# Linear attention feeding a gated feed-forward block: the first pairs reordered across queues and PSUM banks

## The chip, the cores and the metric

The kernel runs on one core of one Trainium2 chip. Five engines with queues of their own work on it: TensorE (PE: matrix products; PEld is its weight load), VectorE (DVE), ScalarE (ACT), GpSimd (POOL, used here for set-up only) and SyncE (SP), which issues every DMA. The metric is device time in microseconds. Three runs of the kernel before took 1288.86, 1289.1 and 1289.23 us, a median of 1289.1 us.

## The reference

Q, K and V have 8 batches of 8 heads, 576 positions and 64 features, in float32; `w_phi` is 64 by 128. Positive random features are made of Q and K, attention is linear, and its output, 4608 tokens of 512 features, passes a feed-forward block of width 1536.

```python
def phi(x):
    proj = einsum('bhsd,df->bhsf', x, w_phi)
    proj = proj - max(abs(proj), axis=-1)
    return concatenate([exp(proj), exp(-proj)], axis=-1)
q_p, k_p = phi(q), phi(k)
kv  = einsum('bhsf,bhsd->bhfd', k_p, v)
z   = sum(k_p, axis=2)
num = einsum('bhsf,bhfd->bhsd', q_p, kv)
den = einsum('bhsf,bhf->bhs', q_p, z)[..., None] + 1e-06
x   = (num / den), heads side by side: 4608 x 512
out = (sigmoid(x @ w_gate) * (x @ w_val)) @ w_out
```

## The kernel before

**Stages.** A pair is two heads of one batch; there are 32 pairs in `steps`, four to a batch. Stage 1 does the attention of all pairs, and between their steps the feed-forward block for the first 4 of 12 slices of its width (`JA`), in 18 chunks of 256 tokens. Its sums go to DRAM (`yscr`). Stage 2 (`rest_chunks`) does the other 8 slices in nine chunks of 512 tokens and adds the stored part. In the feed-forward block each operand is split into a high and a low part (`xh`, `xl`, `wh`, `wl`, `hh`, `hl`), and each product is three matmuls.

**Who sets the order.** In stage 1 everything runs in the order in which the Python code emits it, on each engine by itself (`manual_schedule`). Work that needs several engines in turn is written as generators: `start(g)` runs one to its first `yield`, `tick()` moves every running generator on by one step. What a generator emits in a later tick stands further back in its engine's queue.

**One pair.** `keys` (L477) projects K for two heads into two PSUM banks (L423) and starts `k_exp` (L429): the largest absolute value (`mx`, L434), the subtraction (`dk`, L447) and two exponentials per head on ScalarE (`ek`, L456), one step each. `q_half` (L404), called twice, projects half of Q (L413), and `copies` has ScalarE bring it to `d` (L475). `rest` (L481) does the 64 last positions of both heads (L484) and, from pair `EARLY` = 4 on, lets VectorE add the exponentials of K over three of the position tiles first (`k_sum`, L461: `s` at L469 and `su` at L470, twice a pair). `q_max` (L494) takes the largest absolute value of Q's features on VectorE: a transposing reduction (`pm`, L502), small copies across partitions (`pn`, L507 to L513), a transpose back (`mb`, L515) and the subtraction in `d` (L520). `q_exp` (L560) makes both exponentials (L566). `kv` (L522) accumulates K's features with V (40 matmuls, L530) and the sum z (L544: 40 matmuls from the exponentials, or 16 from `su`) in one bank, which ScalarE copies out (`kvt`, L549). `turn` (L552) transposes it (L556) and copies it out (`kv`, L558). `num` (L571) multiplies with Q's features (`nm`, L582), and for the denominators (`dp`, L593); ScalarE copies the results (`ex`, L599, and `dr`, L609).

**Normalising.** `norm` (L612) sends the denominators through a DMA to a narrow tile, adds 1e-6 and takes reciprocals there, stores them to DRAM (`dens`) and loads them back spread over the partitions (`rb`), each step some ticks after the one before. `num(i, True)` ("soon") instead makes them from `dp` at once, in a tile of full width (L604, L605); before, only pair 3 does. `scale` (L633) multiplies, and stores the result (`xscr`). For batch 0 it also writes the split of x straight into the first chunks' tiles (`split`, L61), and no load follows.

**Banks.** PSUM has eight banks here: two in `ps_gv` for gate and value products, one in `ps_acc` for the output sums, five in `ps_a`. Before, every attention product takes one of the five from `ps_a` (`bank`, L364), and a bank comes free when its last reader has passed.

**The loops.** The first loop (L731) runs pairs 0 to 3 with no feed-forward work. The main loop (L759) starts with the projections of pair 4 and calls `fill` four times a step. `fill` counts spots, adds to `due` what a spot should carry (what is `ready`, spread over the spots left, at most `RATE`), and emits units as `due` allows, with three ticks each time. A unit is half a gate product (`half`, L239) or an output sum (`half_out`, L254); `gate` (L219) is its part on ScalarE and VectorE (L226 to L236). `queue(b)` (L708) makes batch b's chunks due `LAG` spots later. `half` waits, by ticking, until its chunk's x and its weights have been emitted. `weigh` (L669) turns the weights of 12 tiles from 64-bit numbers to high and low parts by `weight_tile` (L121), as far as `grant` allows. After the last pair the remaining units follow without attention between them (L789).

Of the kernel before, what the change touches and what calls it, by code (L numbers as in the profile page):

```python
# [36 lines left out]
EARLY = NP  # L37
RATE = 2.8
LAG = (2, 8)
# [5 lines left out]
def attention_moe(  # L45
# [75 lines left out]
    def weight_tile(w, raw, mid, wp, sp):  # L121
        j, m = divmod(w, 3)
        n = f"{j}_{m}"
        if m == 0:
            weights[j] = tuple(
                wp.tile([P, 3 * DM], F32R, tag=f"w{x}{j}", name=f"w{x}{j}") for x in "hl"
            )
        h, l = (x[:, m * DM : m * DM + DM] for x in weights[j])
        hi = raw.rearrange("p (n two) -> p n two", two=2)[:, :, 1]
        words = mid.rearrange("p (n two) -> p n two", two=2)  # L130
        rest, unit = words[:, :, 0], words[:, :, 1]
        top = sp.tile([P, DM], U32, tag="wtop", name="wtop" + n)
        vec.tensor_scalar(top, hi, 0x7FFFFE00, None, op0=ALU.bitwise_and)
        act.activation(top, top, AF.Relu, bias=ebias, scale=8.0)
        vec.tensor_scalar(rest, rest, 0x01FFFFFF, None, op0=ALU.bitwise_and)
        yield
        vec.scalar_tensor_tensor(
            top, hi, 0x80000000, top, op0=ALU.bitwise_and, op1=ALU.bitwise_or
        )
        nc.sync.dma_start(h.bitcast(U32), top)  # L140
        yield
        vec.tensor_scalar(unit, top, 0xFF800000, None, op0=ALU.bitwise_and)
        vec.scalar_tensor_tensor(
            l, rest, 2.0**-36, unit.bitcast(F32), op0=ALU.mult, op1=ALU.mult
        )
# [208 lines left out]
    with ExitStack() as actx:  # L354
# [9 lines left out]
        def bank(shape, name):  # L364
            return ps_a.tile(shape, F32, tag="a", name=name)
# [14 lines left out]
        steps = [(b, p) for b in range(B) for p in range(NP)]  # L380
# [23 lines left out]
        def q_half(i, hf):  # L404

            n = f"{i}_{hf}"
            if hf == 0:
                ds[i] = at.tile([P, 2, S], F32, tag="d", name=f"d{i}")
# [9 lines left out]
        def k_heads(i):  # L418
            kx = loaded["k", i]
            pps = [bank([P, 4, F], f"pk{i}_{hd}") for hd in range(2)]  # L420
# [60 lines left out]
        def rest(i):  # L481
# [4 lines left out]
            def go():  # L486
                yield from k_exp(i, (2,), [pp], 1)
                if i >= EARLY:
                    yield
                    yield from k_sum(i)  # L490
# [3 lines left out]
        def q_max(i):  # L494
# [6 lines left out]
            mb = at.tile([P, 2, S], F32, tag="mb", name=f"mb{i}", bufs=1)  # L501
# [12 lines left out]
            yield  # L514
            vec.transpose(  # L515
# [6 lines left out]
        def kv(i):  # L522
# [3 lines left out]
            kvz = bank([P, 3 * F], f"kvz{i}")  # L526
# [25 lines left out]
        def turn(i):  # L552
            kvt = kvs[i]
            tp = bank([P, 3, P], f"tp{i}")
# [5 lines left out]
        def q_exp(i):  # L560
            yield
            d = ds.pop(i)
            es = []
            for sg in range(2):
                e = at.tile([P, 2, S], F32, tag=f"eq{sg}", name=f"eq{i}_{sg}", bufs=1)
                act.activation(e, d, AF.Exp, scale=1.0 - 2.0 * sg)  # L566
                es.append(e)
                yield
            exps[i] = es

        def num(i, soon=False):  # L571
# [5 lines left out]
            dps = [bank([P, HS], f"dp{i}_{hf}") for hf in range(1 + soon)]  # L577
            for hf in range(2):
                cs = slice(hf * HS, hf * HS + HS)
                for sg in range(2):  # L580
                    for o in range(0, P, Q):
# [4 lines left out]
                        )  # L586
            for n, dp in enumerate(dps):
# [10 lines left out]
            for hf in range(2):  # L598
                act.copy(ex[:, hf * HS : hf * HS + HS], nms[hf])  # L599
            if soon:  # L600
                rb = at.tile([P, S], F32, tag="mb", name=f"rb{i}", bufs=1)
                for hf, dp in enumerate(dps):
                    cs = slice(hf * HS, hf * HS + HS)
                    vec.tensor_scalar(rb[:, cs], dp, 1e-6, None, op0=ALU.add)  # L604
                    vec.reciprocal(rb[:, cs], rb[:, cs])  # L605
                start(scale(i, ex, rb))
# [5 lines left out]
        def norm(i, ex, dr):  # L612
# [16 lines left out]
            for _ in range(4):  # L629
                yield  # L630
            yield from scale(i, ex, rb)

        def scale(i, ex, rb):  # L633
            b, p = steps[i]
            xp = at.tile([P, S], F32, tag="xp", name=f"xp{i}")
            vec.tensor_tensor(xp, ex, rb, op=ALU.mult)
            for c in range(S // CH if b == 0 else 0):
# [3 lines left out]
                ps = slice(p * CH, p * CH + CH)  # L641
                split(xs[c][0][:, ps], xs[c][1][:, ps], xp[:, c * CH : c * CH + CH])
                parts[c] += 1
            yield
# [80 lines left out]
        N = len(steps)  # L725
# [5 lines left out]
        for i in range(-1, EARLY):  # L731
            load(i + 2 if i >= 0 else N)
            if i + 1 < EARLY:
                keys(i + 1)
                copies(q_half(i + 1, 0))
                tick()
                tick()
                copies(q_half(i + 1, 1))
                rest(i + 1)
                start(q_max(i + 1))  # L740
                tick()
                tick()
            if i >= 0:
                kv(i)
                start(q_exp(i))
            if i >= 1:
                num(i - 1)
            tick()
            tick()
# [121 lines left out]
```

## Time and profile before

| | us |
|---|---|
| median of three runs | 1289.1 |
| the profiled execution's own time | 1289.85 |
| its span, first to last instruction | 1288.1 |
| TensorE busy in the span | 1221.7 |
| VectorE busy | 798.1 |
| ScalarE busy | 525.4 |
| mean granted TensorE clock, share of full | 0.973 |

The profile is one execution. Its first part gives each engine's busy time; its second cuts the span into 40 slices of 32.2 us, where a digit is a busy share in tenths. Groups of instructions stand by line, engine and tile, with their shapes, count, busy time, mean duration in ns, and the engine's idle time just before them with the instruction that ended it. A tile name on the left of an arrow is written, those on the right are read. One matmul call of float32 operands can show as several instructions, so the counts of L413 and L423 are twice those of the calls. Matmuls overlap, so one matmul's duration is longer than its share of the time; in the chain of waits the pieces do not overlap.

### The profile page before, as it was taken

The numbers are of one execution on the slowest core, as the hardware profiler recorded it, in microseconds if no ns is written. First come the engines' busy times: TensorE is split into PE (matmuls) and PEld (weight loads), VectorE is DVE, ScalarE is ACT, GpSimd is POOL, SyncE is SP. The second block draws the span as 40 slices with busy tenths as digits, with TensorE's granted clock in tenths as the row PEclk, the third lists the DMA queues.
The fourth block names the chain that finished last, engine by engine and source line by source line (L and its number), as shares of the span: only waits on it lengthen the run. The fifth ranks groups of instructions, "written<-read, shape, count | busy, mean of one in ns | idle before, by whom it ended". The sixth has DMA issues, their size and how long they took to land.

```text
span 1288.1 us, 22464 instructions
## 1 busy us (share of the span) xinstructions
PE 1221.7 (95%) x9120; PEld 964.7 (75%) x9120; DVE 798.1 (62%) x1608; ACT 525.4 (41%) x1081; POOL 0.7 (0%) x6
## 2 busy tenths in 40 slices
PE   6847799999999999999899999999999999999998
PEld 4435566777787777776798888888888888888886
DVE  7699887888878778884796943434342434333333
ACT  5535556565655656664444322222122222222221
POOL 0000000000000000000000000000000000000000
PEclk8968899999999999999899999999999999999999
DMA  4556334333442433431674530302020201111010
GB/s 176 181 185 236 104 108 138 114 118 105 137 129 84 129 108 110 119 116 58 240 236 169 192 98 1 99 1 92 8 84 15 67 31 57 42 44 56 9 58 33
DMA packets 80869, 131.55 MB, mean 102 GB/s; under 512 B 18301, under 2 KB 37885, under 8 KB 80765
## 3 DMA queue, kind: packets, MB, share of 16 engines
q1 hardware_dynamic: 80764, 130.11, 31.3%
q8 instruction: 72, 1.18, 0.4%
q14 instruction: 33, 0.26, 0.1%
HBM read 92.04 MB, written 28.45 MB: 94 GB/s over the span
## 4 chain that ended last, share of the span: by engine, by line
PE 81%; DVE 10%; ACT 3%; DMA 3%; issue 2%; SPq 0%; DVEq 0%; ACTq 0%
PE acc L171 21%; PE g L164 15%; PE v L164 15%; PE gv L164 11%; PE kvz L530 5%; PE nm L582 4%; PE pq L413 2%; PE dp L593 2%; PE pk L423 2%; ACT eq L566 1%; PE kvz L544 1%; DMA wraw<-w_moe 1%; PE pk L484 1%; DMA rb<-den 1%; DVE t L231 1%
## 5 line engine op out<-in xcount | busy, mean ns | idle before, releaser
L164 PE MATMUL gv<-xh,wh 128*128 128x256 f32 x576 | 173.1, 301 | 14.7 <-ACT xh L62 11.9
L171 PE MATMUL acc<-wh,hh 128*128 128x512 f32 x432 | 172.0, 398 | 0.7 <-ACT hh L234 0.7
L171 PE MATMUL acc<-wl,hh 128*128 128x512 f32 x432 | 169.1, 391 | 0.0
L164 PE MATMUL gv<-xl,wh 128*128 128x256 f32 x576 | 166.2, 289 | 2.8 <-DVE xl L211 2.8
L171 PE MATMUL acc<-wh,hl 128*128 128x512 f32 x432 | 168.7, 390 | 0.0
L164 PE MATMUL gv<-xh,wl 128*128 128x256 f32 x576 | 165.6, 287 | 0.0
L183 DVE TENSOR_SCALAR t<-t 128x512 uint32<-128x512 uint32 x72 | 30.7, 426 | 171.8 <-ACT t L180 171.7
L164 PEld LDWEIGHTS gv<-xh,wh 128*128 128x128 f32 x576 | 112.8, 196 | 32.0 <-issue 14.9
L62 ACT CAST hh<-u 128x512 fp32r<-128x512 f32 x72 | 44.6, 619 | 219.2 <-DVE u L185 219.2
L180 ACT ACTIVATE t<-g 128x512 f32<-128x512 f32 x72 | 43.0, 597 | 183.9 <-PE g L164 183.8
L164 PEld LDWEIGHTS gv<-xl,wh 128*128 128x128 f32 x576 | 113.0, 196 | 3.8 <-DVE xl L211 3.0
L164 PE MATMUL g<-xh,wh 128*128 128x512 f32 x288 | 113.0, 392 | 0.0
L164 PEld LDWEIGHTS gv<-xh,wl 128*128 128x128 f32 x576 | 113.0, 196 | 0.0
L164 PE MATMUL v<-xh,wh 128*128 128x512 f32 x288 | 112.6, 391 | 0.0
L164 PE MATMUL g<-xh,wl 128*128 128x512 f32 x288 | 112.5, 391 | 0.0
L164 PE MATMUL g<-xl,wh 128*128 128x512 f32 x288 | 112.5, 391 | 0.0
L164 PE MATMUL v<-xl,wh 128*128 128x512 f32 x288 | 112.3, 390 | 0.0
L164 PE MATMUL v<-xh,wl 128*128 128x512 f32 x288 | 112.1, 389 | 0.0
L184 DVE SCALAR_TENSOR_TENSOR t<-t,v 128x512 f32<-128x512 f32 x72 | 49.4, 686 | 97.9 <-PE v L164 97.9
L171 PEld LDWEIGHTS acc<-wh,hh 128*128 128x128 f32 x432 | 81.1, 188 | 22.4 <-issue 4.8
L171 PEld LDWEIGHTS acc<-wh,hl 128*128 128x128 f32 x432 | 81.1, 188 | 18.7 <-DVE hl L236 0.2
L171 PEld LDWEIGHTS acc<-wl,hh 128*128 128x128 f32 x432 | 81.3, 188 | 16.0
(92 smaller groups left out, 2114.1 us busy)
## 6 DMA issues: line engine op xcount, KB each, us to landing
wraw<-w_moe SPq DMA_DIRECT2D x36, 512.0 KB, 5.7
xl<-xs SPq DMA_DIRECT2D x34, 512.0 KB, 4.1
k<-k SPq DMA_DIRECT2D x32, 320.0 KB, 3.7
v<-v SPq DMA_DIRECT2D x32, 320.0 KB, 3.0
q<-q SPq DMA_DIRECT2D x32, 288.0 KB, 4.3
wh<-wtop SPq DMA_DIRECT2D x36, 256.0 KB, 2.3
ys<-y SPq DMA_DIRECT2D x36, 256.0 KB, 2.0
yp<-ys SPq DMA_DIRECT2D x36, 256.0 KB
```

What stands on the lines that cost most here:

```text
L62: a = act.copy(h, x)
L164: nc.tensor.matmul(o, a[:, ws], x[:, cs], start=i == 0, stop=i == 11)
L171: nc.tensor.matmul(acc, a[:, ts], w[:, ws], start=first and i == 0, stop=last and i == 2)
L180: act.activation(t, g, AF.Tanh, scale=0.5)
L183: vec.tensor_scalar(tu, tu, 0x7FFFFFFF, None, op0=ALU.bitwise_and)
L184: vec.scalar_tensor_tensor(t, t, 1.0, vl, op0=ALU.add, op1=ALU.mult)
L231: vec.scalar_tensor_tensor(t, t, 1.0, gv[:, 1, :], op0=ALU.add, op1=ALU.mult)
L413: nc.tensor.matmul(pps[hd], wk[head(hd), :], x[head(hd), cs], start=True, stop=True)
L423: nc.tensor.matmul(pps[hd][:, t, :], kx[head(hd), t * P : t * P + P], wk[head(hd), :], start=True, stop=True,)
L530: nc.tensor.matmul(kvz[o : o + Q, : 2 * F], vx[:, 2 * t + hd, o % D : o % D + Q], (e0, e1)[hd][:, t, :] if t < 4 else e2[:, 0, :], start=t ...
L582: nc.tensor.matmul(nms[hf][o : o + Q, :], w[:, sg, o : o + Q], es[sg][:, o // D, cs], start=sg == 0, stop=sg == 1, tile_position=(0, o),)
L593: nc.tensor.matmul(dp[o : o + Q, :], w[:, 2, z : z + Q], es[sg][:, hd, hf * HS : hf * HS + HS], start=sg == 0, stop=sg == 1, tile_position ...
```

## The change

- `ONPE` = 10: `k_sum` is used from pair 10 on instead of pair 4, so pairs 4 to 9 sum K's features with 40 matmuls.
- `LAG` goes from (2, 8) to (4, 8).
- `weight_tile` gains a step: the mask of `rest` is emitted ahead of the Relu, and the Relu one tick later.
- For the first pairs `bank` takes other pools: K's projections of pairs 0 to 4 the two gate banks, `kvz` and its transpose of pairs 0 to 3 the one output bank.
- `d` has three buffers. Q's second exponential is written over `d`, the first has two buffers. For pairs 0 to 3 `q_exp` emits both at once, right after the copies of the next pair, ahead of `kv`.
- `num` copies each half of `nm` as soon as its matmuls are emitted, and takes the banks of `dp` after that. With `soon`, the addition and the reciprocal are made in the bank, and `scale` multiplies from it.
- `norm` waits two ticks instead of four after loading `rb`, for pairs 0 to 3.
- `scale` casts x one tick after the product, and subtracts one tick after that.
- The first loop takes in the projections of pair 4 and pair 3's `num`; the main loop starts at pair 4. In its last two steps `fill` is called where the projections would stand. The last pair (31) is done with `soon`.

```diff
+ONPE = 10
-LAG = (2, 8)
+LAG = (4, 8)
...
         vec.tensor_scalar(top, hi, 0x7FFFFE00, None, op0=ALU.bitwise_and)
+        vec.tensor_scalar(rest, rest, 0x01FFFFFF, None, op0=ALU.bitwise_and)
+        yield
         act.activation(top, top, AF.Relu, bias=ebias, scale=8.0)
-        vec.tensor_scalar(rest, rest, 0x01FFFFFF, None, op0=ALU.bitwise_and)
         yield
...
-        def bank(shape, name):
+        def bank(shape, name, i=N, ps=None, tag=None):
+            if i < EARLY:
+                return ps.tile(shape, F32, tag=tag, name=name)
             return ps_a.tile(shape, F32, tag="a", name=name)
...
-                ds[i] = at.tile([P, 2, S], F32, tag="d", name=f"d{i}")
+                ds[i] = at.tile([P, 2, S], F32, tag="d", name=f"d{i}", bufs=3)
...
-            pps = [bank([P, 4, F], f"pk{i}_{hd}") for hd in range(2)]
+            pps = [bank([P, 4, F], f"pk{i}_{hd}", i - 1, ps_gv, "gv") for hd in range(2)]
...
-                if i >= EARLY:
+                if i >= ONPE:
                     yield
                     yield from k_sum(i)
...
-            kvz = bank([P, 3 * F], f"kvz{i}")
+            kvz = bank([P, 3 * F], f"kvz{i}", i, ps_acc, "acc")
...
-            tp = bank([P, 3, P], f"tp{i}")
+            tp = bank([P, 3, P], f"tp{i}", i, ps_acc, "acc")
...
         def q_exp(i):
-            yield
+            if i >= EARLY:
+                yield
             d = ds.pop(i)
-            es = []
-            for sg in range(2):
-                e = at.tile([P, 2, S], F32, tag=f"eq{sg}", name=f"eq{i}_{sg}", bufs=1)
-                act.activation(e, d, AF.Exp, scale=1.0 - 2.0 * sg)
-                es.append(e)
-                yield
-            exps[i] = es
+            e = at.tile([P, 2, S], F32, tag="eq", name=f"eq{i}")
+            act.activation(e, d, AF.Exp)
+            if i >= EARLY:
+                yield
+            act.activation(d, d, AF.Exp, scale=-1.0)
+            exps[i] = e, d
+            yield
...
+                act.copy(ex[:, cs], nms[hf])
+            dps = [bank([P, HS], f"dp{i}_{hf}") for hf in range(1 + soon)]
...
-            for hf in range(2):
-                act.copy(ex[:, hf * HS : hf * HS + HS], nms[hf])
             if soon:
-                rb = at.tile([P, S], F32, tag="mb", name=f"rb{i}", bufs=1)
-                for hf, dp in enumerate(dps):
-                    cs = slice(hf * HS, hf * HS + HS)
-                    vec.tensor_scalar(rb[:, cs], dp, 1e-6, None, op0=ALU.add)
-                    vec.reciprocal(rb[:, cs], rb[:, cs])
-                start(scale(i, ex, rb))
+                for dp in dps:
+                    vec.tensor_scalar(dp, dp, 1e-6, None, op0=ALU.add)
+                    vec.reciprocal(dp, dp)
+                start(scale(i, ex, dps))
                 return
...
-            for _ in range(4):
+            for _ in range(4 if i >= EARLY else 2):
                 yield
...
-            vec.tensor_tensor(xp, ex, rb, op=ALU.mult)
+            for n, rb in enumerate(rbs):
+                cs = slice(n * w, n * w + w)
+                vec.tensor_tensor(xp[:, cs], ex[:, cs], rb, op=ALU.mult)
+            if b == 0:
+                yield
...
-                split(xs[c][0][:, ps], xs[c][1][:, ps], xp[:, c * CH : c * CH + CH])
+                act.copy(
+                    xs[c][0][:, p * CH : p * CH + CH], xp[:, c * CH : c * CH + CH]
+                )
+            yield
+            for c in range(S // CH if b == 0 else 0):
+                xh, xl = (x[:, p * CH : p * CH + CH] for x in xs[c])
+                vec.tensor_tensor(
+                    xl, xp[:, c * CH : c * CH + CH], xh.bitcast(F32), op=ALU.subtract
+                )
                 parts[c] += 1
...
         for i in range(-1, EARLY):
             load(i + 2 if i >= 0 else N)
-            if i + 1 < EARLY:
-                keys(i + 1)
-                copies(q_half(i + 1, 0))
-                tick()
-                tick()
-                copies(q_half(i + 1, 1))
-                rest(i + 1)
-                start(q_max(i + 1))
-                tick()
-                tick()
+            keys(i + 1)
+            copies(q_half(i + 1, 0))
+            copies(q_half(i + 1, 1))
+            rest(i + 1)
+            start(q_max(i + 1))
+            tick()
             if i >= 0:
+                start(q_exp(i))
                 kv(i)
-                start(q_exp(i))
+            tick()
+            tick()
             if i >= 1:
                 num(i - 1)
-            tick()
-            tick()
             if i >= 0:
                 turn(i)
                 load_v(i + 2)
-            tick()
-            tick()
+            if i == EARLY - 1:
+                num(i, True)
+            for _ in range(3):
+                tick()
             grant(i)
-        num(EARLY - 1, True)
-        grant(6)
         queue(0)
-        for i in range(EARLY - 1, N + 1):
-            if EARLY <= i:
-                load(i + 2)
-                grant(3 * (i - 1))
+        for i in range(EARLY, N + 1):
+            load(i + 2)
+            grant(3 * (i - 1))
...
+            else:
                 fill()
-            if i < EARLY:
-                fill()
-                fill()
-                continue
+            fill()
             if i < N:
                 kv(i)
             if i > EARLY:
-                num(i - 1)
+                num(i - 1, i == N)
```

More of the change, by code (lines that the diff above doesn't have):

```diff
@@ L362, in attention_moe @@
         ps_acc = actx.enter_context(tc.tile_pool(name="ps_o", bufs=1, space=PSUM))
-        def bank(shape, name):
+        steps = [(b, p) for b in range(B) for p in range(NP)]
+        N = len(steps)
+        def bank(shape, name, i=N, ps=None, tag=None):
+            if i < EARLY:
+                return ps.tile(shape, F32, tag=tag, name=name)
             return ps_a.tile(shape, F32, tag="a", name=name)
@@ L379, in attention_moe @@
         ]
-        steps = [(b, p) for b in range(B) for p in range(NP)]
         loaded, ks, ds, exps, kvs, rbs = {}, {}, {}, {}, {}, {}
@@ L500, in q_max @@
             pn = at.tile([P, nj], F32, tag="pn", name=f"pn{i}")
-            mb = at.tile([P, 2, S], F32, tag="mb", name=f"mb{i}", bufs=1)
             vec.tensor_reduce(
@@ L514, in q_max @@
             yield
+            mb = at.tile([P, 2, S], F32, tag="mb", name=f"mb{i}", bufs=1)
             vec.transpose(
@@ L560, in q_exp @@
         def q_exp(i):
-            yield
-            d = ds.pop(i)
-            es = []
-            for sg in range(2):
-                e = at.tile([P, 2, S], F32, tag=f"eq{sg}", name=f"eq{i}_{sg}", bufs=1)
-                act.activation(e, d, AF.Exp, scale=1.0 - 2.0 * sg)
-                es.append(e)
-                yield
-            exps[i] = es
+            if i >= EARLY:
+                yield
+            d = ds.pop(i)
+            e = at.tile([P, 2, S], F32, tag="eq", name=f"eq{i}")
[4 more added lines that the diff above has]
+            exps[i] = e, d
+            yield
         def num(i, soon=False):
@@ L576, in num @@
             nms = [bank([P, HS], f"nm{i}_{hf}") for hf in range(2)]
-            dps = [bank([P, HS], f"dp{i}_{hf}") for hf in range(1 + soon)]
             for hf in range(2):
@@ L628, in norm, with scale @@
                 )
-            for _ in range(4):
+            for _ in range(4 if i >= EARLY else 2):
                 yield
-            yield from scale(i, ex, rb)
-        def scale(i, ex, rb):
+            yield from scale(i, ex, [rb])
+        def scale(i, ex, rbs):
             b, p = steps[i]
             xp = at.tile([P, S], F32, tag="xp", name=f"xp{i}")
-            vec.tensor_tensor(xp, ex, rb, op=ALU.mult)
+            w = S // len(rbs)
+            for n, rb in enumerate(rbs):
[3 more added lines that the diff above has]
+                yield
             for c in range(S // CH if b == 0 else 0):
@@ L640, in scale @@
                     xs[c] = x_tiles(moe, CH, f"1_{c}")[:2]
-                ps = slice(p * CH, p * CH + CH)
-                split(xs[c][0][:, ps], xs[c][1][:, ps], xp[:, c * CH : c * CH + CH])
+                act.copy(
[7 more added lines that the diff above has]
+                )
                 parts[c] += 1
-            yield
             t = 0
@@ L723, in grant @@
                 wdone += 1
-        N = len(steps)
         for i in range(2):
```

## The prediction, made before the change was run

> **What bounds the kernel now.** First the page: its span, and busy tenths and granted TensorE clock in 40 slices.
>
> ```profile
> span 1288.1 us, 22464 instructions
> PE   6847799999999999999899999999999999999998
> DVE  7699887888878778884796943434342434333333
> PEclk8968899999999999999899999999999999999999
> ```
>
> TensorE (PE) is busy nearly everywhere from the sixth slice (160 us) on; only the first five slices show holes, a lower clock, and VectorE (DVE) at 6 to 9 tenths. The windows view puts numbers on it (columns: length, busy us of PE, weight loads, VectorE, ScalarE, GpSimd; granted clock, DMA share, GB/s).
>
> ```profile
> 17.80:66.92 49.12, 40.12 (x614) 24.40 (x614) 36.32 (x73) 29.53 (x61) 0.00 (x0) 0.92 0.42 139
> 66.92:164.50 97.58, 68.75 (x665) 49.02 (x666) 87.66 (x192) 47.90 (x108) 0.00 (x0) 0.80 0.55 177
> 0.00:164.50 164.50, 116.81 (x1331) 79.22 (x1332) 134.88 (x289) 83.25 (x181) 0.70 (x6) 0.84 0.53 175
> 164.50:240.00 75.50, 70.37 (x732) 49.76 (x731) 60.46 (x130) 44.95 (x98) 0.00 (x0) 0.95 0.42 124
> 240.00:280.00 40.00, 40.00 (x471) 30.25 (x474) 33.44 (x77) 24.32 (x57) 0.00 (x0) 1.00 0.38 119
> ```
>
> From 240 us TensorE is the bound without a hole, so what happens there costs or saves exactly its TensorE work. Before 164.5 us TensorE idles 164.5 - 116.81 = 47.7 us. In 66.92 to 164.5 VectorE is busy 87.66 of 97.58 us, 90%: **it is the bound there**. In 17.8 to 66.92 it idles 12.8 us. The waits view of TensorE, 60 to 160 us, names who comes last.
>
> ```profile
> PE pq L413 <- ACT d L475: 14.6, 5, 5.3
> PE gv L164 <- ACT xh L62: 11.9, 2, 8.4
> PE kvz L530 <- issue: 3.1, 1, 3.1
> ```
>
> The 11.9 us are the first MoE halves (a half: the 12 matmuls of one gate or value product), placed in the code ahead of pair 4's attention, waiting for pairs 3 and 2 to be normalised and cast. The 14.6 us are Q's projections waiting for a PSUM bank that ScalarE (ACT) has not copied out, ScalarE itself standing behind something VectorE makes.
>
> **A checkpoint.** I take the end of `d -= max` (L520) of pair 8. The windows view of L520, then that of L164, to 164.5 us:
>
> ```profile
> 0.00:164.50 164.50, 12.19 (x9) 0.84 0.53 175
> 0.00:164.50 164.50, 27.34 (x157) 24.07 (x158) 0.84 0.53 175
> ```
>
> The ninth L520 is pair 8's and ends at 164.5 us; by then 157/12 = 13.1 MoE halves have started. All 12 weight tiles are cast by it in both kernels (four ticks a tile after, twelve ticks a pair: two tiles in the first loop, then three a pair, the twelfth in pair 7's step). So the question is what VectorE must do up to there, and how long it stands. Its groups to 164.5 us:
>
> ```profile
> L469 DVE TENSOR_TENSOR s<-ek 128x512 f32<-128x512 f32 x10 | 6.8, 681 | 0.0
> L470 DVE TENSOR_TENSOR su<-s 128x256 f32<-128x256 f32 x9 | 3.8, 425 | 0.3
> L232 DVE SCALAR_TENSOR_TENSOR u<-u,t 128x256 f32<-128x256 f32 x6 | 2.6, 426 | 0.2
> L231 DVE SCALAR_TENSOR_TENSOR t<-t,gv 128x256 f32<-128x256 f32 x6 | 2.5, 422 | 0.8
> L236 DVE TENSOR_TENSOR hl<-u,hh 128x256 fp32r<-128x256 f32 x6 | 2.5, 409 | 0.9 <-ACT hh L234 0.9
> L230 DVE TENSOR_SCALAR t<-t 128x256 uint32<-128x256 uint32 x6 | 1.6, 265 | 1.1 <-ACT t L226 1.1
> L434 DVE TENSOR_REDUCE mx<-pk 128x4 f32<-128x512 f32 (+1 forms) x27 | 14.0, 547 | 5.9 <-PE pk L423 5.1 <-PE pk L484 0.7
> L502 DVE TRANSPOSE_TENSOR_REDUCE pm<-d 128x36 f32<-128x1152 f32 x9 | 12.4, 1374 | 4.6 <-ACT d L475 4.5
> ```
>
> **The change, part by part.**
>
> *K's sums on TensorE for pairs 4 to 9 (ONPE).* VectorE loses 6.8 + 3.8 = 10.6 us before the checkpoint. TensorE does 40 matmuls instead of 16 for z (L544); from the chain of waits, with two rows for later:
>
> ```profile
> 27.64 2.29 PE kvz L530 x40
> 29.94 1.09 PE kvz L544 x40
> 45.81 0.48 PE tp L556 x3
> 142.43 0.44 PE kvz L544 x16
> ```
>
> That is 1.09 - 0.44 = 0.65 us a pair. Pairs 4 to 7 lie beside a VectorE that is the bound: nothing, and 4 x 0.65 = 2.6 us if that cover goes. Pairs 8 and 9 are paid: 1.3 us.
>
> *The reordered first loop: pair 4's keys and queries join it, MoE starts two fills later (LAG 4, and the count starts later), Q's exponentials go straight behind the copies, banks are split.* No matmul or exponential is added. The dead stretch goes: TensorE's 8.4 us before the first halves, and VectorE's early idling. The banks: kvz(0) started at 17.80 us although its exponentials were done, in the same instant as VectorE's first `dk` of pair 1 gave a bank back (timeline):
>
> ```profile
> 17.02 1.28 DVE L447 TENSOR_TENSOR dk<-pk,mx 128x512 f32<-128x512 f32 x2
> 17.77 0.23 PEld L530 LDWEIGHTS kvz<-ek,v 128*32 128x32 f32 x8 [4.96 <-issue]
> ```
>
> With K's projections in the gate banks it can start up to 4.8 us sooner, if v has landed (between 0 and 4.8 us; nothing of it counts by itself, VectorE being the longer row). The new single bank for kvz and its transpose makes kvz(i+1) wait for ScalarE's copy of kv(i). ScalarE's order per pair becomes four d copies, two Q exponentials, kvt, K's exponentials, ex, dr, kv; whatever the Q exponentials wait for now also holds K's. I followed the three queues by hand through pairs 0 to 3. K and Q preparation costs VectorE about 8.7 us a pair (for nine pairs L434 14.0 and L447 as much, L502 12.4 and L515 and L520 as much each, and some 13 of small ops). ScalarE's 29.53 us of the second window are about three and a half pairs, 8.4 each; TensorE's 40.12 are four, 10 each. They overlap; TensorE waits some 5 us for kv(3) before num(3), and VectorE meets dp(3) with about 2 us of idling, where L604 waited 4.87 (row below). VectorE's 12.8 us of idling in that window can stay whole or go whole; I keep 2 beside dp(3)'s 2, since by hand its row had no other gap.
>
> *The gates behind.* MoE now falls due at spot 4, at (28.7 us of units)/26 spots = 1.10 us a spot, a half being entered at 1.45: 0.76 halves a spot. Pair 8's L520 is in spot 15, so 11 spots or 8.4 halves precede it. About two gates fewer lie on VectorE: 2 x (2.6 + 2.5 + 2.5 + 1.6)/6 = 3 us. But 13.1 - 8.4 = 4.7 halves must be made up later by TensorE. A half at full clock, and one at the low clock (chain of waits):
>
> ```profile
> 564.95 1.42 PE gv L164 x12
> 96.22 2.56 PE gv L164 x12
> ```
>
> 4.7 x 1.42 = 6.7 us.
>
> *Weights' Relu one tick later, x's casts one step behind.* Same instructions; VectorE issues the mask first and stops waiting for ScalarE inside a step (a gain of at most a few us, in the idling below). Unseen here: the multiply by `rb` after two ticks instead of four for pairs 0 to 2. VectorE is in order, so a late `rb` holds all behind it, K's maxima and weight casts. The DMA view (0 to 140 us; last number us to landing):
>
> ```profile
> rb<-den SPq DMA_DIRECT2D x8, 144.0 KB, 6.5
> ```
>
> Between 0 and 3 x 6.5 = 19.5 us. By my count about 8 us of VectorE work lie between reciprocal and multiply, so I take 1 us each.
>
> *Reciprocals in the bank* (pair 3, and now 31). The timeline:
>
> ```profile
> 60.84 0.46 DVE L604 TENSOR_SCALAR rb<-dp 128x288 f32<-128x288 f32 x1 [4.87 <-PE dp L593]
> 61.33 1.95 DVE L605 RECIPROCAL rb<-rb 128x288 f32<-128x288 f32 x1
> 615.65 0.75 DVE L636 TENSOR_TENSOR xp<-ex,rb 128x576 f32<-128x576 f32 x1
> ```
>
> I keep 1.95 us with a bank on both sides; no row shows that form, and half or double it is -2 to +4 us on VectorE for pair 3. For pair 31 it replaces two DMA hops. What the tail can give (its last dp in the chain of waits, then the waits of TensorE, 540 to 700 us):
>
> ```profile
> 601.62 1.15 PE dp L593 x16
> ```
>
> ```profile
> PE gv L164 <- ACT xh L209: 2.8, 1, 2.8
> PE gv L164 <- DVE xl L211: 2.8, 1, 2.8
> PE nm L582 <- ACT eq L566: 2.1, 2, 1.7
> ```
>
> Two fills now stand ahead of num(31), so 2.1 goes. Pair 31's product came at 615.65; by the bank it comes at 602.8 + 1.0 for the second half of dp + 2 x (0.46 + 1.95) = 608.6, some 7 us sooner. But more MoE has been done inside the loop by then, so less work covers it: I take 1 of the 5.6. That half of dp costs 1.0. Net 2.1.
>
> **The sum.** The first mx in the timeline:
>
> ```profile
> 6.39 1.29 DVE L434 TENSOR_REDUCE mx<-pk 128x4 f32<-128x512 f32 x2 [5.11 <-PE pk L423]
> ```
>
> VectorE to the checkpoint: 134.9 - 10.6 - 3 = 121.3 us. Idling: 6.4 until the first mx (6.39), 2 at dp(3), and for the rest, `rb` included, the 10% of 66.92 to 164.5 us taken on the 63 us that follow the first loop, 6.3, plus 2 for the first loop: 17. Checkpoint at 138.3 instead of 164.5: -26.2. Made up later: +6.7 (halves), +1.3 (z). From 164.5 to 240 us TensorE idled 5.1; with VectorE lighter for pairs 8 and 9 I take half: -2.5. Tail -2.1. **Total -22.8 us, 1.8%.** The profiled execution took 1289.85 us, 1.75 around its span and 0.75 over the median of 1289.1 us; against the median that is **1266.3 us**.
>
> *A rule weighed.* After the 8.4 us hole the halves ran at 2.56 us instead of 1.42, and 66.92 to 164.5 us was granted 0.80. The Trainium skill (TensorE: Matmul & The Clock Gate, "Why this matters for your kernels") says that a TensorE pause of more than about 3 us drops the array to half clock until it has been busy about as long again. By that rule the change, which leaves such pauses while VectorE is the bound, keeps paying after each. The trace agrees in kind; whether it decides is the second rival below.
>
> **The rivals.**
>
> 1. *VectorE never stands*: idling only 6.4 + 2, checkpoint at 129.7, all 5.1 us after it gone: -34.8 + 8.0 - 5.1 - 2.1 = -34.0, **1255**. For it: VectorE at 90% already. Against: three in-order engines of nearly equal load.
> 2. *TensorE stays at the low clock and becomes the bound of pairs 4 to 7*: 8.4 halves x 1.14 and the rest in proportion, 12 us given back: **1278**. Against: TensorE has 68.75 us of work in 97.58 today, with fewer halves later.
> 3. *`rb` arrives late for all three pairs*: 16.5 us beyond my 3: **1283**. For it: the 6.5 us row; against: SyncE is issuing other work meanwhile.
> 4. *Slower: the first loop becomes one chain* through the single kvz bank and ScalarE, kv(i) copied only after K's exponentials and ex. It decides when the checkpoint is no earlier than about 161 us, which needs 5.7 us more per early pair than VectorE's 8.7. Not earlier at all, it costs 6.7 + 1.3 + 2.6 - 2.5 - 2.1 = +6.0: **1295**. Against: kvz, z and the transpose (2.29 + 1.09 + 0.48) and ScalarE's 8.4 laid end to end make 12.3, not 14.4.
> 5. *No change*: the holes only move behind pair 4, about **1289**.
>
> **Chances.** Forecast (1258 to 1274) 0.50; rival 1 (1247 to 1258) 0.17; rival 2 0.10; rival 3 (both 1274 to 1286) 0.13; rival 4 0.06; rival 5 0.04. Range: 1250 to 1281, leaving out the far ends of rivals 1 and 3 and all of 4 and 5, about 0.2. Within 0.2% (2.6 us) is what a measurement here cannot tell from no change: faster 0.90, same 0.04, slower 0.06.
>
> **What would show it.** Nine L520 ended by about 138 us; L469 44 times instead of 56; kvz(0) before 17.8 us; no hole of 8 us ahead of the first gv; TensorE full from about 150 us; nm's wait on eq gone in the tail; stage 2 untouched. I am wrong if VectorE shows waits on the `rb` DMA of several us, if kvz waits on kv's copy in each early pair, or if TensorE still has holes at 200 us.

## The result and the profile after

The changed kernel took 1276.49 us, the median of four runs (1275.16 to 1278.25), against 1288.98 us (1287.96 to 1289.23) for the kernel before: a ratio of 0.9905, with a 95% interval of 0.9888 to 0.9923. That is 12.5 us less, where 22.8 were forecast: the sign and the range held, the size was 0.55 of it. The time lies above the forecast's own band (1258 to 1274 us), in the one that the prediction gave to rivals 2 and 3 with a chance of 0.23.

From the page of the changed kernel: its span, the busy tenths and granted clock in 40 slices, and TensorE's costliest group (the last row's idle time is in TensorE, before L173).

```profile
span 1274.3 us, 22722 instructions
PE   7648899999999999999989999999999999999998
DVE  7678878888877878884996843434343424343333
PEclk9868899999999999999998999999999999999999
L173 PE MATMUL acc<-wh,hh 128*128 128x512 f32 x432 | 173.3, 401 | 6.9 <-ACT y L265 3.5
```

The picture is the one of before with its first part shortened: TensorE has holes in the first five slices and hardly any later. Stage 2 is untouched: its first product of 512 tokens starts at 691.09 us before and at 677.27 us after, 13.8 us earlier, and both spans end 13.8 us apart (1288.1 and 1274.3). The two profiled executions lie a little to either side of their medians, hence 13.8 here and 12.5 between medians.

The windows view of the changed kernel answers to that of before. The checkpoint, the end of pair 8's `d -= max` (now L527, started at 150.51 us, 1.36 long), stands at 151.87 us. Columns as before: length, busy us and instructions of PE, weight loads, VectorE, ScalarE, GpSimd; granted clock, DMA share, GB/s.

```profile
0.00:151.87 151.87, 106.78 (x1367) 72.47 (x1368) 121.83 (x264) 79.67 (x173) 0.70 (x6) 0.85 0.58 188
151.87:240.00 88.13, 87.29 (x994) 66.10 (x995) 70.32 (x156) 54.42 (x121) 0.00 (x0) 1.00 0.38 116
17.80:66.92 49.12, 36.24 (x556) 22.37 (x556) 38.26 (x83) 29.35 (x66) 0.00 (x0) 0.90 0.36 112
66.92:151.87 84.95, 60.06 (x679) 42.24 (x680) 72.84 (x157) 42.09 (x91) 0.00 (x0) 0.80 0.65 211
```

The checkpoint came 12.6 us earlier (164.5 before). **VectorE's work up to it was forecast at 121.3 us and measured 121.83. Its idling was forecast at 17 us and measured 151.87 - 121.83 = 30.0 us**, as much as before (164.5 - 134.88 = 29.6). So all that the checkpoint gained is work taken off VectorE; the idling that was to go was replaced by other idling. The waits view of VectorE, 0 to 151.87 us, says by what (total us, times, longest):

```profile
DVE xp L644 <- DMA rb<-den: 14.6, 4, 6.4
DVE mx L441 <- PE pk L430: 5.3, 2, 5.1
DVE dp L609 <- PE dp L602: 3.4, 1, 3.4
```

That row at the top is `scale`'s product (L644) waiting for the reciprocals to come back from DRAM; in the kernel before no product waited for `rb` in this stretch. Three of its four waits are those of pairs 0, 1 and 2 (6.41, 3.51 and 2.69 us, 12.6 in all), where the prediction put 3 us. The fourth is pair 4's, which keeps its four ticks and which the prediction did not count:

```profile
127.09 0.76 DVE L644 TENSOR_TENSOR xp<-ex,rb 128x576 f32<-128x576 f32 x1 [2.00 <-DMA rb<-den]
```

The timeline of SyncE, which issues the DMAs, in the stretch of the first such wait (start, duration, line):

```profile
35.43 0.33 SPq L627 DMA_DIRECT2D den<-dn  x1
40.29 0.53 SPq L142 DMA_DIRECT2D wh<-wtop  x1
40.92 1.18 SPq L408 DMA_DIRECT2D v<-v  x1
42.15 0.42 SPq L114 DMA_DIRECT2D wraw<-w_moe  x1
42.87 0.33 SPq L116 DMA_DIRECT2D wmid<-w_moe  x1
43.29 1.15 SPq L631 DMA_DIRECT2D rb<-den  x2
```

The denominators' store goes out at 35.43 us, the load that brings them back spread over the partitions at 43.29: eight microseconds in which SyncE's queue stood in order behind other transfers. The timeline of VectorE shows what those transfers waited for:

```profile
35.19 0.21 DVE L625 RECIPROCAL dn<-dn 128x9 f32<-128x9 f32 x1
...
39.58 0.68 DVE L139 SCALAR_TENSOR_TENSOR wtop<-wraw,wtop 128x512 uint32<-128x512 uint32 x1
...
42.03 0.82 DVE L145 SCALAR_TENSOR_TENSOR wl<-wmid 128x512 fp32r<-128x512 uint32 x1
42.77 1.34 DVE L527 TENSOR_TENSOR d<-d,mb 128x1152 f32<-128x1152 f32 x1
50.52 0.76 DVE L644 TENSOR_TENSOR xp<-ex,rb 128x576 f32<-128x576 f32 x1 [6.41 <-DMA rb<-den]
```

The store of `wh` needs L139's result, ready at 40.26 us, and goes out at 40.29. The load of `wmid` overwrites what L145 reads, done at 42.85, and goes out at 42.87. Both stand in VectorE's queue between the reciprocal and the product that needs `rb`. **The 8 us of VectorE work that were counted as cover for the transfer were what held the transfer back**: only when they were done did SyncE get to the load, and VectorE, with nothing left ahead of the product, stood for the whole way of the data. The waits view of SyncE, 0 to 100 us, has the same pattern in total:

```profile
SPq L142 <- DVE wtop L139: 16.5, 3, 7.0
SPq L408 <- PE kvz L537: 13.0, 2, 7.3
SPq L116 <- DVE wl L145: 9.7, 2, 9.5
```

The second time the queue holds the load longer. Pair 1's denominators were stored at 53.70 us and loaded back only at 70.84, because `wmid`'s load (70.42) waited for an L145 that VectorE reached at 69.70, behind pair 3's long reciprocals. Then VectorE stood 3.51 us more, until 75.84.

### The profile page after: what moved, and what is told of

The parts are those of the page before. It is cut to its first block, busy times and chain, and to the rows that moved or that the text cites. A ratio compares the mean times of both kernels' runs of the same rounds, so it can differ in the third digit from the quotient of the medians.

```text
span 1274.3 us, 22722 instructions
## 1 busy us (share of the span) xinstructions
PE 1216.5 (95%) x9280; PEld 964.8 (76%) x9280; DVE 788.3 (62%) x1588; ACT 524.5 (41%) x1080; POOL 0.7 (0%) x6
## 4 chain that ended last, share of the span: by engine, by line
PE 84%; DVE 9%; DMA 4%; issue 1%; ACT 1%; SPq 0%; DVEq 0%; ACTq 0%
PE acc L173 22%; PE g L166 16%; PE v L166 15%; PE gv L166 13%; PE kvz L537 5%; PE nm L589 4%; PE pq L420 3%; PE pk L430 2%; PE dp L602 2%; DMA rb<-den 2%; PE kvz L551 1%; DMA wraw<-w_moe 1%; PE pk L491 1%; DVE mb L522 1%; PE tp L563 1%
## 5 line engine op out<-in xcount | busy, mean ns | idle before, releaser
L173 PE MATMUL acc<-wh,hh 128*128 128x512 f32 x432 | 173.3, 401 | 6.9 <-ACT y L265 3.5
L166 PE MATMUL gv<-xh,wh 128*128 128x256 f32 x576 | 170.5, 296 | 3.5 <-ACT xh L651 3.5
L173 PE MATMUL acc<-wl,hh 128*128 128x512 f32 x432 | 170.1, 394 | 0.0
L173 PE MATMUL acc<-wh,hl 128*128 128x512 f32 x432 | 169.8, 393 | 0.2 <-DVE hl L238 0.2
L166 PE MATMUL gv<-xl,wh 128*128 128x256 f32 x576 | 163.5, 284 | 4.0 <-DVE xl L657 3.5
L166 PE MATMUL gv<-xh,wl 128*128 128x256 f32 x576 | 163.1, 283 | 0.0
L166 PEld LDWEIGHTS gv<-xh,wh 128*128 128x128 f32 x576 | 110.4, 192 | 20.8 <-issue 14.5
L166 PEld LDWEIGHTS gv<-xl,wh 128*128 128x128 f32 x576 | 110.5, 192 | 4.9 <-DVE xl L657 3.8
L166 PE MATMUL g<-xh,wh 128*128 128x512 f32 x288 | 113.0, 392 | 0.0
L166 PE MATMUL v<-xh,wh 128*128 128x512 f32 x288 | 112.6, 391 | 0.0
L166 PE MATMUL g<-xh,wl 128*128 128x512 f32 x288 | 112.5, 391 | 0.0
L166 PE MATMUL g<-xl,wh 128*128 128x512 f32 x288 | 112.5, 391 | 0.0
L166 PE MATMUL v<-xl,wh 128*128 128x512 f32 x288 | 112.3, 390 | 0.0
L166 PE MATMUL v<-xh,wl 128*128 128x512 f32 x288 | 112.1, 389 | 0.0
L166 PEld LDWEIGHTS gv<-xh,wl 128*128 128x128 f32 x576 | 110.3, 192 | 0.0
L173 PEld LDWEIGHTS acc<-wh,hh 128*128 128x128 f32 x432 | 81.8, 189 | 31.5 <-issue 6.7
L173 PEld LDWEIGHTS acc<-wh,hl 128*128 128x128 f32 x432 | 81.6, 189 | 19.4 <-DVE hl L238 0.7
L173 PEld LDWEIGHTS acc<-wl,hh 128*128 128x128 f32 x432 | 81.9, 190 | 16.2
```

What stands on the lines that cost most here:

```text
L166: nc.tensor.matmul(o, a[:, ws], x[:, cs], start=i == 0, stop=i == 11)
L173: nc.tensor.matmul(acc, a[:, ts], w[:, ws], start=first and i == 0, stop=last and i == 2)
```

## The experiments

Two theories. **The queue**: the lateness of `rb` for pairs 0 to 2 costs its full length, because VectorE sets the checkpoint, and its cause is the order in SyncE's queue. **The parts**: the idling is there anyway (the first loop is a chain of three engines), with `rb` in time VectorE waits elsewhere, and the size is off because single parts of the change were mis-sized. All kernels below compute the full result and start from the changed kernel. Medians of four to eleven runs each, ratios against runs of the kernel before on the same chip; the last column is the end of pair 8's L527 in the profiled execution (L526 in `e9_relu`, L520 before).

| label | edit to the changed kernel | us | ratio, 95% interval | checkpoint |
|---|---|---|---|---|
| (before) | | 1288.98 | 1 | 164.5 |
| (after) | none | 1276.49 | 0.9905 [0.9888, 0.9923] | 151.9 |
| e1_rb4 | four ticks before the product for all pairs | 1275.87 | 0.9892 [0.9874, 0.9911] | 150.6 |
| e2_rbpool | `rb` of pairs 0 to 2 loaded on GpSimd's queue | 1266.78 | 0.9822 [0.9804, 0.9841] | 142.4 |
| e7_normpool | all three hops of pairs 0 to 2 there | 1266.43 | 0.9829 [0.9810, 0.9847] | 143.0 |
| e12_pool3 | as e7, and three ticks instead of two | 1262.87 | 0.9798 [0.9780, 0.9816] | 140.4 |
| e10_poollag6 | as e7, and LAG (6, 8) | 1265.56 | 0.9814 [0.9794, 0.9834] | 142.1 |
| e11_poolksum8 | as e7, and ONPE 8 | 1266.72 | 0.9826 [0.9808, 0.9844] | 143.0 |
| e3_ksum4 | K's sums as before (ONPE 4) | 1282.78 | 0.9949 [0.9932, 0.9966] | 157.5 |
| e6_lag2 | LAG (2, 8) as before | 1287.83 | 0.9990 [0.9977, 1.0002] | 157.6 |
| e5_last | pair 31 normalised as before | 1280.38 | 0.9935 [0.9920, 0.9950] | 152.6 |
| e4_banks | banks as before | 1276.91 | 0.9902 [0.9883, 0.9920] | 151.1 |
| e8_qlate | Q's exponentials behind K's, as before | 1277.86 | 0.9920 [0.9903, 0.9938] | 154.0 |
| e9_relu | weights' Relu with the first mask, as before | 1277.46 | 0.9907 [0.9890, 0.9925] | 150.2 |

**Is it the wait for `rb`?** First its place in VectorE's queue (e1), then its place in the DMA queue (e2).

```diff
-            for _ in range(4 if i >= EARLY else 2):
+            for _ in range(4):
```

> One edit: the multiply by rb waits four ticks again for pairs 0 to 2, as before the change. Theory A (the forecast gain was lost in VectorE's waits for the rb DMA, 14.6 us before pair 8's d, in a stage where VectorE is the bound): two more ticks of VectorE work stand ahead of the multiply, the waits for rb fall from 14.6 us to under 6, and the time to 1268 to 1272 us. Theory B (those waits lie in slack that TensorE or ScalarE would have spent anyway): the waits fall but the time stays within 1274 to 1279 us. Theory C (casts and the first MoE halves are late then, since x of chunk 0 comes two ticks later): slower, 1278 to 1283 us.

```diff
-                nc.sync.dma_start(
+                (nc.sync if i >= EARLY else pool).dma_start(
```

> One edit: for pairs 0 to 3 the two loads of rb are issued by GpSimd's queue, which is empty, instead of SyncE's; the two ticks stay. Theory A with SyncE as the cause (rb is issued behind wh's store, which waits for VectorE, v's load, which waits for kvz, and the raw weights, 5 to 8 us after den was stored): rb is issued about 2 us after den, the waits for rb fall below 4 us in all, the time to 1265 to 1270 us. Rival (the latency of the load itself, about 6 us, is the cause, wherever it is issued): waits stay above 10 us, time 1274 to 1278.

With four ticks the wait for `rb` is all but gone, and nothing is gained (0.6 us, inside the intervals). The waits view of VectorE in `e1_rb4`, 0 to 151 us:

```profile
DVE dn L624 <- DMA dn<-dr: 9.8, 4, 4.3
DVE dp L609 <- PE dp L602: 5.4, 1, 5.4
DVE mx L441 <- PE pk L430: 5.0, 1, 5.0
...
DVE xp L644 <- DMA rb<-den: 0.3, 1, 0.3
```

A good part of what had stood at the product now stands at the next pair's first hop, `dn`, whose load follows `rb`'s in SyncE's queue (43.49 us and 44.73 us in this trace): 6.1 of the 9.8 us are pairs 1 and 2, the rest pairs 4 and 5; `dp`'s wait is 2.0 us longer too. Taken by itself this looks like the second theory: the idling is there anyway. But with `rb` on a queue of its own 9.7 us go, and the checkpoint comes 9.5 us earlier: one for one. The waits view of VectorE in `e2_rbpool`, 0 to 151 us, has a third of the wait left:

```profile
DVE mx L441 <- PE pk L430: 5.3, 2, 5.1
DVE xp L644 <- DMA rb<-den: 4.5, 2, 2.3
DVE dp L609 <- PE dp L602: 2.3, 1, 2.3
...
DVE dn L624 <- DMA dn<-dr: 1.4, 1, 1.4
```

So the first theory holds, put more exactly: it is not the number of ticks that made `rb` late but SyncE's queue, and any hop of the normalising that passes through that queue can stand in it. On GpSimd's queue the data also landed sooner (last section); the two effects were not separated.

**What is left of the wait, and can the kernel be had faster?** All three hops on GpSimd's queue (e7), and then one tick more (e12):

```diff
-            nc.sync.dma_start(dn, dr.rearrange("(o r) c -> o r c", r=Q)[:, 0, :])
+            dq = nc.sync if i >= EARLY else pool
+            dq.dma_start(dn, dr.rearrange("(o r) c -> o r c", r=Q)[:, 0, :])
...
-            nc.sync.dma_start(dens[i].rearrange("h (r c) -> (h r) c", c=9), dn)
+            dq.dma_start(dens[i].rearrange("h (r c) -> (h r) c", c=9), dn)
...
-                nc.sync.dma_start(
+                dq.dma_start(
...
-            for _ in range(4 if i >= EARLY else 2):
+            for _ in range(4 if i >= EARLY else 3):
```

The last two lines are e12's alone.

> All three hops of norm (dn, den, rb) of pairs 0 to 2 on GpSimd's queue, two ticks kept. In the run with rb alone moved, 4.5 us of waits for rb and 1.4 for dn were left. If SyncE's order is still behind them (dn is issued behind the raw weights and xs): both fall below 3 us in all, 1263 to 1266 us. If what is left is the way of the data itself: no change to that run, 1266 to 1268 us.

> Norm's hops on GpSimd's queue, and three ticks instead of two ahead of the multiply. In the run with two, VectorE still waited 4.9 us for rb. If those are real idle time of the bound: they go, 1262 to 1265 us. If what stands behind the multiply (casts of x, the first halves) then comes late instead: 1266 to 1270 us.

e7 is no faster than e2: moving the two small hops as well takes the wait for `dn` away and leaves 4.9 us at `rb`. Of these, 2.3 are pair 4's, whose hops go through SyncE's queue in all these kernels, and 2.6 are pair 2's. As I read it, the way of pair 2's data (a store, a load) is longer than the work that two ticks leave in between; e12 bears that out, since there pair 2's product no longer waits and the checkpoint comes 2.6 us earlier. The third tick pays now, where in e1 more ticks paid nothing: 3.6 us over e7, 13.6 over the changed kernel, 26 us or 2.0% over the kernel before. In `e12_pool3` the waits view of VectorE, 0 to 150 us, begins:

```profile
DVE mx L441 <- PE pk L430: 6.5, 2, 5.1
DVE dp L609 <- PE dp L602: 3.5, 1, 3.5
DVE xp L645 <- DMA rb<-den: 2.7, 1, 2.7
```

The 2.7 us left at `rb` are again pair 4's; moving its hops too was not tried. The windows row up to the checkpoint is

```profile
0.00:140.35 140.35, 110.23 (x1367) 73.53 (x1368) 121.39 (x264) 80.18 (x173) 7.88 (x18) 0.88 0.63 204
```

121.39 us of VectorE work, the same as in the changed kernel, and 19.0 us of idling, where 17 had been forecast: with the queue out of the way the forecast's picture of the start is nearly there.

**The parts that were to gain.** K's sums (e3), LAG (e6), the last pair (e5):

```diff
-ONPE = 10
+ONPE = 4
```

> One edit: ONPE 4, so VectorE sums K's features for pairs 4 to 9 again, 2.2 us a pair, and TensorE has 0.65 us a pair less. If VectorE bounds pairs 4 to 8 (Theory A): about 8 to 11 us more VectorE work before pair 8's d and 3.9 us less on TensorE after, net 1281 to 1285 us. If TensorE is the bound there (Theory B): about 3 us faster, 1272 to 1274 us.

6.3 us slower. Up to the checkpoint the sums that come back take 10.0 us (6.19 and 3.82), all of VectorE's work is 8.4 us more (130.22), and its idling is 27.3 us instead of 30.0, with 12.5 instead of 14.6 at `rb`: so the checkpoint comes 5.6 us later. Which other work was less was not looked into.

```diff
-LAG = (4, 8)
+LAG = (2, 8)
```

> One edit to the changed kernel: LAG (2, 8), so the first MoE units fall due at spot 2, before kvz(4). Theory A (VectorE is the bound there and chunk 0's x is not ready at spot 2): ticks are forced, TensorE waits for x ahead of kvz(4) and pair 5's start moves back, 1278 to 1284 us. Rival (TensorE has holes of 7 us there anyway, two halves earlier fill them): 1273 to 1276 us.

11.3 us slower, more than the whole range expected. The waits view of TensorE in `e6_lag2`, 60 to 160 us, begins with

```profile
PE gv L166 <- ACT xh L651: 12.9, 2, 8.8
PE gv L166 <- DVE xl L657: 6.2, 2, 3.5
```

and that of the changed kernel over the same stretch has

```profile
PE kvz L537 <- issue: 9.0, 2, 7.3
PE pq L420 <- ACT d L482: 5.1, 2, 3.1
PE gv L166 <- DVE xl L657: 3.5, 1, 3.5
PE gv L166 <- ACT xh L651: 3.5, 1, 3.5
```

With the old LAG the first MoE halves again stand at the head of TensorE's queue before their x is cast, 19.1 us in place of 7.0. The checkpoint comes 5.7 us later, nearly all of it as idling of VectorE: 35.4 us up to it instead of 30.0. By what way the halves cause that is argued, not shown: no single row grows by so much. Waits for ScalarE's `wtop`, `d` and `t` are 1.9, 1.5 and 0.9 us longer and that for `wmid`'s load 1.1, while those for TensorE's `pk` and `dp` are 0.9 longer together. Besides, 9.0 halves have started by then instead of 9.75, which is 1.1 us; and TensorE idles 2.6 us from there to 240 us instead of 0.8. That accounts for 8.6 of the 11.3 us; the rest was not traced.

```diff
-                num(i - 1, i == N)
+                num(i - 1)
```

> One edit to the changed kernel: pair 31 goes through norm and its DMAs again instead of making its reciprocals in the bank; the extra fills in the last steps stay. The prediction put the whole tail at 2.1 us, of which the bank's part was 0 (1 us of waits against 1 us of TensorE for the second half of dp). Theory A (the bank's part is worth nothing, TensorE waits for other things there): 1275 to 1278 us. Rival (x of the last chunk comes some 7 us later and TensorE, now with less work to cover it, waits): 1279 to 1284 us.

3.9 us slower. The waits view of TensorE, 540 to 700 us, first in the changed kernel, then in `e5_last`:

```profile
PE acc L173 <- ACT y L265: 3.5, 1, 3.5
PE acc L173 <- ACT hh L236: 3.4, 2, 2.2
PE gv L166 <- DVE xl L213: 0.5, 1, 0.5
PE acc L173 <- DVE hl L238: 0.2, 1, 0.2
```

```profile
PE gv L166 <- ACT xh L211: 3.5, 1, 3.5
PE gv L166 <- DVE xl L213: 3.3, 1, 3.3
PE acc L173 <- ACT y L265: 2.1, 1, 2.1
PE acc L173 <- ACT hh L236: 2.1, 2, 1.2
```

The waits add up to 8.4 us before (2.8, 2.8, 2.1, 0.7), 11.0 in e5 and 7.6 after. The reciprocals in the bank take away nearly all of the wait for x, 6.8 us in e5, and waits of the output sums for ScalarE's `hh` and `y` give a part of it back.

**Parts that were to do nothing by themselves.** The banks (e4), the place of Q's exponentials (e8), the weights' Relu (e9):

```diff
-            pps = [bank([P, 4, F], f"pk{i}_{hd}", i - 1, ps_gv, "gv") for hd in range(2)]
+            pps = [bank([P, 4, F], f"pk{i}_{hd}") for hd in range(2)]
...
-            kvz = bank([P, 3 * F], f"kvz{i}", i, ps_acc, "acc")
+            kvz = bank([P, 3 * F], f"kvz{i}")
...
-            tp = bank([P, 3, P], f"tp{i}", i, ps_acc, "acc")
+            tp = bank([P, 3, P], f"tp{i}")
```

> One part undone: K's projections, kvz and its transpose take the five shared banks for all pairs. The prediction gave this part nothing by itself, since VectorE has the longer row: 1275 to 1279 us, with kvz(0) back at about 17.8 us instead of 12 to 13. Rival: the shared banks tie TensorE to ScalarE's copies in the first pairs, VectorE loses its unbroken row in pairs 0 to 3 (8.5 us apart), and the time rises by 5 us or more, 1281 to 1287 us.

```diff
             if i >= 0:
-                start(q_exp(i))
                 kv(i)
             tick()
             tick()
+            if i >= 0:
+                start(q_exp(i))
             if i >= 1:
                 num(i - 1)
```

> One part undone: in the first loop Q's two exponentials are started after K's exponentials of the next pair, ahead of num, instead of straight behind the copies of d. If their place between the copies carries the gain: kv's copies and num come later, pairs 0 to 3 lengthen, 1280 to 1286 us. If it does not (VectorE's row is unbroken either way; ScalarE's order only shifts): 1274 to 1278 us. If K's exponentials behind Q's were the cost (they stand behind a wait for VectorE's d): faster, 1270 to 1274 us.

```diff
         vec.tensor_scalar(top, hi, 0x7FFFFE00, None, op0=ALU.bitwise_and)
-        vec.tensor_scalar(rest, rest, 0x01FFFFFF, None, op0=ALU.bitwise_and)
-        yield
         act.activation(top, top, AF.Relu, bias=ebias, scale=8.0)
+        vec.tensor_scalar(rest, rest, 0x01FFFFFF, None, op0=ALU.bitwise_and)
         yield
```

> One part undone: the weights' Relu is issued with the first mask again, three ticks a tile. Theory A (SyncE's order in the first 100 us is what costs): wh's stores and the raw loads stand elsewhere between norm's hops, so the waits for rb change, by up to 5 us either way, 1271 to 1281 us. Rival (the extra step carries part of the gain by itself, VectorE no longer waiting for ScalarE inside a tile): 3 us or more slower, with waits of wtop on the Relu back at 3 us.

0.4, 1.4 and 1.0 us, all within the intervals. The first `kvz` starts at 12.5 us in the changed kernel and at 13.8 in e4, against 17.80 before. So the bank that gave the change a part of its name accounts for 1.3 of those 5.3 us and for nothing at the end, since VectorE's row is the longer one there.

**Going on in the same direction** once the queue is out of the way:

```diff
-LAG = (4, 8)
+LAG = (6, 8)
```

> Norm's hops of pairs 0 to 2 on GpSimd's queue, and LAG (6, 8): the first MoE halves two fills later still. With LAG 2 the time was 11 us worse than with 4. If 4 still comes too early (TensorE waits 7 us for x of chunk 0 ahead of pair 5's keys): 1261 to 1264 us. If x is ready by then and only the halves are missing later, when TensorE is the bound: 1267 to 1271 us.

```diff
-ONPE = 10
+ONPE = 8
```

> Norm's hops on GpSimd's queue, and ONPE 8: pairs 8 and 9 sum K's features on VectorE again. If VectorE is the bound only to pair 8's d, as the prediction had it: 1.3 us of TensorE saved, 1264 to 1266 us. If VectorE is still behind in pairs 8 and 9: up to 4 us slower, 1267 to 1270 us.

Neither differs from e7 by what the runs can tell (-0.9 and +0.3 us). In e10 the waits for x at the head of the first halves are gone from TensorE's view, but 10.1 us for `d` have come in place of 5.1: after LAG 4 the next wait is ScalarE's.

## Why the prediction came out as it did

**What bounds the kernel: right.** The end follows the checkpoint. Median minus checkpoint is 1124.5 us before and 1124.6 after, and lies between 1122.5 (e12) and 1127.3 (e9) over checkpoints from 140.4 to 164.5; only e6 (1130.3) stands out, for the reasons above, and e5, which changes the tail, is left out of this.

**VectorE's work: right.** 10.6 us of K's sums and 3 us of gates were taken off; 121.83 us stayed where 121.3 were forecast. L476, which was L469, runs 44 times.

**The step that failed: "I take 1 us each" for `rb`.** Bounds of 0 and 19.5 us were given, the working took 3, and those three pairs waited 12.6: 9.6 of the 13.0 us by which the idling exceeded its forecast. Pair 4's 2.0, put at nothing, and `dp`'s 3.4 instead of 2 come next. Two things were wrong in it. The 6.5 us row holds one hop, the load; ahead of it goes the store, and in e12 the first loads are issued 2.0, 4.0 and 2.4 us after that. And above all, SyncE's order was not followed. Rival 3 says against itself that SyncE "is issuing other work meanwhile": that was the cause, not a reason against it. The weights' store and load ahead of it each had to wait for a VectorE instruction that stands between the reciprocal and the product. Rival 3's mechanism is thus the one that happened, at 9.6 of its 16.5 us, and waits on `rb` of several us are what the prediction had named as a sign of being wrong. That 22.8 less 9.7 (e2) is 13.1, beside 12.5 measured, is partly luck: e2's checkpoint is still 4.1 us behind the forecast's 138.3, and the halves and the idling behind the checkpoint, below, were mis-sized the other way.

**The reordered first loop: as followed by hand.** Pairs 0, 1 and 2 end L527 at 15.88, 24.39 and 32.91 us, 8.5 apart where 8.7 was worked out. From 17.8 to 66.92 us VectorE idles 49.12 - 38.26 = 10.9 us; the first wait for `rb` (6.41) taken off leaves 4.5, forecast 4. That the loop becomes one chain (rival 4) did not happen. Nothing here was undone by itself except Q's place and the banks; taking pair 4's projections out of the first loop was not tried.

**LAG: the largest of the parts undone one at a time, and not priced by itself.** The prediction put it under the idling. 11.3 us hang on it.

**The gates behind: right in kind.** 9.75 halves have started at the checkpoint (117 matmuls of L166 at 12 a half; 8.4 forecast, 13.1 before). 3.3 halves at 1.42 us are 4.7 us to make up, not 6.7. Behind the checkpoint TensorE idled 0.8 us to 240 us where it had idled 5.1: 4.3 us gained, forecast 2.5.

**The tail: wrong in its parts and in its net.** `nm`'s wait of 2.1 us went. The wait for x fell from 5.6 to 0.5 us, where 1 of the 5.6 had been taken, and new waits for `y` and `hh` of 6.9 us against 0.7 were not foreseen. The waits fell by 0.8 us where 3.1 were forecast, and the second half of `dp` costs the 1.0 us that was forecast, so by these the tail gave nothing, where a net of 2.1 was forecast; without the reciprocals in the bank the waits would have grown, to 11.0 (e5). Why the output sums now wait for ScalarE was not looked into. The form without a row, the reciprocal with a bank on both sides, was taken at 1.95 us and took 1.97:

```profile
594.67 1.97 DVE L610 RECIPROCAL dp<-dp 128x288 f32<-128x288 f32 x1
```

**The sum by the trace:** -12.6 (checkpoint) + 4.7 (halves) + 1.3 (z of pairs 8 and 9, 1.09 us each instead of 0.44, as forecast) - 4.3 (idling behind the checkpoint) - 1.7 (all of TensorE's idling from 240 us to stage 2, 9.3 us before and 7.6 after) + 1.0 (second half of `dp`) = -11.6 us. The checkpoint gave 13.6 us less than forecast; the halves and the idling from it to 240 us came out 3.8 us better, the tail about 2 worse. Between the medians it is -12.5, between the two profiled executions -13.8; about 2 us of the latter were not traced.

**The rivals.** Rival 1 (VectorE never stands) asked for 8.4 us of idling and had 30. Rival 2 (the low clock decides) did not happen: from 66.92 us to the checkpoint the granted clock is 0.80 as before, but TensorE has 60.06 us of work in 84.95, and moving a DMA took 9.7 us off while the granted clock of that stretch stayed at 0.80 (e2). The low clock is there all the same. In TensorE's timeline of the changed kernel, one gate matmul before, behind and well behind a pair of waits of 3.5 us each:

```profile
86.42 0.28 PE L166 MATMUL gv<-xh,wl 128*128 128x256 f32 x1
...
94.84 0.41 PE L166 MATMUL gv<-xh,wh 128*128 128x256 f32 x1
...
99.79 0.28 PE L166 MATMUL gv<-xh,wl 128*128 128x256 f32 x1
```

The starts of one matmul and the next are 0.12, 0.21 and again 0.12 us apart there. The rule of the Trainium skill that the prediction weighed (TensorE: Matmul & The Clock Gate, "Why this matters for your kernels"), half clock after a pause of more than about 3 us, agrees with these rows in kind. Rival 5 (holes only move) is what e1 shows for one hop, and was not the whole.

**One wait read only, not tested.** TensorE's longest hole after is 7.28 us before pair 4's `kvz` at 79.45 us, put down to nothing ("issue"). VectorE's first `dk` of the next pair ends at about 79.4 us, as it did when the first `kvz` was let go before; that `dk` stood behind the product that waited for `rb` until 75.84. It fits that this hole, too, comes from SyncE's queue: in e12 the longest of these is 3.7 us.

## What to carry to other kernels

When work on engine V is counted as cover for a DMA, follow the queue that issues the DMA entry by entry: if an entry ahead of it waits for that very work, the cover is none. A short chain of hops that an in-order engine waits for belongs on a DMA queue in which nothing waits for that engine; give it that queue before you give it more ticks, since ticks alone (e1) moved much of the wait to the next hop and gained nothing. And pick a checkpoint whose distance to the end stays the same: it tells in one number whether a part gains at the place that sets the end.

## What the runs showed of the hardware

GpSimd, idle in this kernel, issues these loads about as fast as SyncE (0.5 us each), and the data arrives sooner. The DMA view, 0 to 140 us, of `e2_rbpool`, last number us from issue to landing:

```profile
rb<-den POOLq DMA_DIRECT2D x6, 144.0 KB, 3.1
```

Before, the same loads of the same size on SyncE's queue had a median of 6.5 us. In the changed kernel the loads just ahead of them on that queue bring 320 KB of V and twice 512 KB of raw weights. The Trainium skill (DMA: Bandwidth & Descriptors, "Issuing engines are not separate DMA queues") has it that starting DMAs on several engines saves only the sequencer's time, which is usually small beside the DMA itself. Here the two kernels that differ in that one queue alone are 9.7 us apart. I read most of it as the order of the sequencer: pair 0's load goes out 1.7 us after its store (36.12, 37.84) instead of 7.9, pair 1's 3.8 instead of 17.1. How much the shorter way of 3.1 us adds was not measured by itself.

A reciprocal of 128 x 288 takes the same with its operand and result in PSUM as in SBUF, 1.97 and 1.95 us.
